# Pooled attention and a top-1 mixture of experts on one core: routing's loads on another queue, 26 filling products, four changes of order

## The chip, the core and the metric

The kernel runs on one core of a Trainium2 chip. The core has five engines with a queue of instructions each: TensorE (PE; its weight loads are shown as PEld), VectorE (DVE), ScalarE (ACT), GpSimd (POOL) and SyncE (SP, which here only issues DMAs and loads registers). Each queue runs in order; an instruction that waits for a semaphore holds all that stand behind it on its engine. ScalarE can issue DMAs as SP can. The metric is the device time of one execution in microseconds.

## What is computed

Inputs are q, k, v of 8 batches x 8 heads x 576 rows x 64, and a mixture of 8 experts of 512 x 1024 x 512. All is float32.

```python
k_p = k.reshape(B, H, Sp, pool, D).mean(axis=3)        # pool 8: 576 rows become 72
v_p = v.reshape(B, H, Sp, pool, D).mean(axis=3)
attn = softmax(scale * q @ k_p.T) ;  x = (attn @ v_p)  # 4608 tokens of 512
logits = x @ w_gate + modality_bias[modality_id]
e_idx = argmax(logits) ;  gate_w = softmax(logits)[e_idx]
out = gate_w * (relu(x @ w1[e_idx]) @ w2[e_idx])
```

## The kernel before, in words

**Attention** is 20 steps of two tiles of 128 query rows (the third of every five, the mixed step with `jj` None, has one tile, of two batches' remainders). Step n works in two halves w of four heads. Its parts are written as functions and called in an order written out by hand, in the loop over n from line 1097 on: `q_pe` (L679) transposes queries on PE into a PSUM tile `pq` of the pool `ps_tr`, which has two buffers, and `q_act` (L685) copies them to SBUF as `qt` on ACT; `s_pe` (L704, L698) makes scores `sc`; `s_dve` (L711, L714) subtracts the maximum on DVE; `s_act` (L726, L727) takes the exponential `pe` on ACT; `t_pe`, `t_act` (L733, L738) transpose it and copy it as `pt`; `t4_pe`, `t4_act` (L745, L752) do so for the remainders; `a_pe` (L768, L772) multiplies with the pooled values into `av`; `x_dve` (L791 to L801) normalises on DVE.

**Pooling** runs a batch or two ahead: `pool_k`, `pool_v` and their `_rest` fold eight rows on POOL (L458 to L460) or reduce on DVE (L463); `k_operand` (L502 to L511) transposes pooled keys on PE and copies them as `kt` on ACT; `v_operand` (L542 to L551) scales pooled values on ACT, and transposes them on PE as `pv`. Where they stand is set by the hooks `hook_0`, `hook_1`, `hook_q`, `hook_2`, `hook_3`, lists of functions for each step, run at five points of it.

**Routing** of a group of nine tiles is a list of small DVE operations, `route(g)`. They wait in the list `drip`, and `gap(n)` puts up to n of them between other DVE operations; an operation on PE in that list (`pe`, in the set `held`) stops `gap` until `release` takes it. POOL's `modality_terms` (L624 to L627), hooked at step 5, turns the modality and its bias into what L852 adds on DVE at step 6; these come by five DMAs of `load_routing` (L583, L585, L588), of 512, 256, 512, 256 and 128 rows of 32, 8, 32, 8 and 64 bytes.

**Loads.** Before the change SP issues all plain DMAs, in the order of `load_...` calls and of `step_loads`. Each DMA signals its landing on one of eight counters (DMAHW0 to DMAHW7), given out in turn to all DMAs in the order of the program, whichever engine issues them; the instruction that issues a DMA waits until the DMA before it on its counter has landed.

**Filling products** (`fill`, L494) are bf16 products of constants on PE that nobody reads.

**The experts** follow: slots of 256 tokens, gathered by POOL, with `first0` and `first_pair` (L193, L236, L240), `second` (L1436); the first expert's first products stand in the last attention steps. `first0` leaves its DVE part, the low part (L210), in the list `rests`, which `finish()` runs.

Of the kernel before, what the change touches and what calls it, by code (L numbers as in the profile page):

```python
# [9 lines left out]
F32 = mybir.dt.float32  # L10
F32R = mybir.dt.float32r
BF16 = mybir.dt.bfloat16
I32 = mybir.dt.int32
# [9 lines left out]
P = 128  # L23
# [11 lines left out]
def kernel(  # L35
# [303 lines left out]
    with ExitStack() as actx:  # L339
# [150 lines left out]
        def fill(n):  # L490

            t = ps_av.tile([P, 2, 512], F32, tag="av", name="fill")
            for _ in range(n):
                nc.tensor.matmul(t[:, 0, 0:P], iota_b, iota_b, start=True, stop=True)  # L494
# [44 lines left out]
        def v_operand(b):  # L539
            vp, vp4 = vps[b]  # L540
            dw, d4 = vw[b % NB], v4[b % NB]
            nc.scalar.activation(dw[:, :, 0, 0:HD], vp[:, 0:NPAIR, :], AF.Copy, scale=m_a)  # L542
            nc.scalar.activation(dw[:, :, 1, 0:HD], vp[:, 0:NPAIR, :], AF.Copy, scale=m_b)
            (nc.gpsimd if b else nc.vector).tensor_tensor(d4[:, :, 0:HD], vp4.rearrange("p (o d) -> p o d", o=1).to_broadcast([P, NPAIR, HD]),
                                    m4b.to_broadcast([P, NPAIR, HD]), op=ALU.mult)

            pv = ps_tr.tile([P, 3, P], F32, tag="tr", name=f"pv_{b}")
            for u in range(3):
                nc.tensor.transpose(pv[:, u, :], vp[:, 2 * u:2 * u + 2, :], ident)
            vts[b] = ap.tile([P, 3, P], F32, tag="vt", bufs=1, name=f"vt_{b}")  # L550
            nc.scalar.copy(vts[b], pv)  # L551

# [21 lines left out]

        RC = {}

        def load_routing():

            mod = ap.tile([P, NT, 2], I32, name="mod")
            mv = modality.bitcast(I32).rearrange("(n w) -> n w", w=2)  # L580
            for z in range(2):
                mz = mv.rearrange("(i z s) w -> z i s w", z=2, s=S)[z]
                nc.sync.dma_start(mod.rearrange("p (i t) w -> p i (t w)", t=GT)[:, :, 10 * z:10 * z + 8],  # L583
                                  mz[:, 0:512, :].rearrange("i (p j) w -> p i (j w)", j=4))
                nc.sync.dma_start(mod.rearrange("p (i t) w -> p i t w", t=GT)[64 * z:64 * z + 64, :, 4, :],  # L585
                                  mz[:, 512:S, :].rearrange("i p w -> p i w"))
            mb = ap.tile([P, 2, E], F32, name="mb")
            nc.sync.dma_start(mb.rearrange("p m e -> p (m e)"),  # L588
                              modality_bias.rearrange("m e -> (m e)").rearrange("(o x) -> o x", o=1).to_broadcast([P, 2 * E]))
            RC.update(mod=mod, mb=mb)  # L590

        def routing_constants():
            ids = ap.tile([P, NT], I32, name="ids")
# [53 lines left out]
        def gap(n=2):  # L647

            for _ in range(n):
                if drip and drip[0] not in held:  # L650
                    drip.pop(0)()
# [31 lines left out]
        def q_act(n, w):  # L683
            pq = pqs.pop((n, w))
            nc.scalar.copy(qts[n, w][:, 0:2 * len(steps[n][2]), :], pq)  # L685
# [18 lines left out]
                    nc.tensor.matmul(dst, qt[:, i, :], kt[b % NB][:, :, h * SPL:(h + 1) * SPL], start=True, stop=True)  # L704
            scs[n, w] = spare[w] = sc

        def s_dve(n, w):
            nh = 2 * len(steps[n][2])
            scv = scs.pop((n, w))[:, :, 0:nh * SPL].rearrange("p u (h s) -> p u h s", s=SPL)
            mx = ap.tile([P, 2, 4], F32, tag="mx", bufs=2, name=f"mx_{n}_{w}")[:, :, 0:nh]  # L710
            nc.vector.reduce_max(mx, scv, axis=AX.X)  # L711
            gap()
            sb = ap.tile([P, 2, 4 * SPL], F32, tag="sb", bufs=2, name=f"sb_{n}_{w}")
            nc.vector.tensor_tensor(sb[:, :, 0:nh * SPL].rearrange("p u (h s) -> p u h s", s=SPL), scv,  # L714
                                    mx.rearrange("p u (h o) -> p u h o", o=1).to_broadcast([P, 2, nh, SPL]), op=ALU.subtract)
            scs[n, w] = sb
# [31 lines left out]
        def t4_act(n):  # L748

            dst = pt4s[n]  # L750
            for z in range(len(steps[n][2])):
                nc.scalar.copy(pt4z[z][64 * z:64 * z + 64], dst[64 * z:64 * z + 64])  # L752
# [18 lines left out]
                for hs, y in halves:  # L771
                    nc.tensor.matmul(dst4[hs], pt4[:, hs], v4[y][:, 2 * u:2 * u + 2, :], start=False, stop=True)  # L772

        def x_dve(t):
            n, z = tile_step[t]
            g, gi = tile_group[t]
            av = avs.pop(t)
            mixed = steps[n][1] is None
            b = steps[n][0]
            if gi == 0:  # L780
                lgs[g] = late_p.tile([P, GT, H, E], F32, tag="lg", bufs=2, name=f"lg_{g}")
            xw = xbs[n if n < NX0 else NX0 + n % (len(xbs) - NX0)]
            xo = xw[:, z, 0:D]
            avv = av[:, :, 0:4 * VC].rearrange("p u (h x) -> p u h x", h=4)
            s8 = ap.tile([P, 2, 4], F32, tag="r", bufs=4, name=f"r_{t}")


            late = g >= EARLY_GROUPS and z == 1
            r = xw[:, z, RX:RX + H].rearrange("p (u h) -> p u h", u=2) if late else s8
            rb = r.rearrange("p u (h o) -> p u h o", o=1)  # L790
            nc.vector.tensor_scalar(s8, avv[:, :, :, VC - 1], float(POOL), 1e-9 * POOL, op0=ALU.mult, op1=ALU.add)  # L791
            if late:
                nc.scalar.copy(xo.rearrange("p (u h d) -> p u h d", u=2, h=4), avv[:, :, :, 0:HD])
            gap(1)
            nc.vector.reciprocal(r, s8)
            gap(1)
            nc.vector.tensor_tensor(lgs[g][:, gi].rearrange("p (u h) e -> p u h e", u=2), avv[:, :, :, HD:HD + E],
                                    rb.to_broadcast([P, 2, 4, E]), op=ALU.mult)
            if not late:
                for u in range(2):  # L800
                    nc.vector.tensor_tensor(xo[:, u * D // 2:(u + 1) * D // 2].rearrange("p (h d) -> p h d", h=4),  # L801
                                            avv[:, u, :, 0:HD], rb[:, u].to_broadcast([P, 4, HD]), op=ALU.mult)
            gap(2)

            if mixed:
                for y in range(2):
                    r0 = (b - 1 + y) * S + 512
                    stores.append(lambda y=y, r0=r0: nc.sync.dma_start(xs[r0:r0 + 64, :], xw[64 * y:64 * y + 64, 0, :]))
            elif z == 1:
                jj = steps[n][1]  # L810
                stores.append(lambda: nc.sync.dma_start(
                    xs[b * S:b * S + 512, :].rearrange("(p j) x -> p j x", j=4)[:, 2 * jj:2 * jj + 2, :], xw))
# [238 lines left out]

        step_loads = {}
        for n, fn, b in ((0, load_k, 2), (0, load_k4, 2), (0, load_v, 2), (0, load_v4, 2), (1, load_q, 2), (1, load_k, 3),
                         (1, load_v, 3), (1, load_k4, 3), (1, load_routing, None), (1, load_k, 4), (2, load_qmix, 1),
                         (2, load_v4, 3), (2, load_v, 4), (3, load_k4, 4), (4, load_q, 3), (4, load_k, 5), (4, load_v4, 4),
                         (4, load_v, 5), (5, load_k4, 5), (5, load_k, 6), (6, load_q, 4), (6, load_v4, 5), (6, load_v, 6),
                         (7, load_qmix, 2), (7, load_k4, 6), (7, load_k, 7), (9, load_q, 5), (9, load_v4, 6), (9, load_v, 7),
                         (10, load_k4, 7), (11, load_q, 6), (11, load_v4, 7), (12, load_qmix, 3), (14, load_q, 7)):
            step_loads.setdefault(n, []).append((fn, b))
# [11 lines left out]
        k_operand(0, 0)  # L1071
        q_pe(0, 0)
        q_act(0, 0)
        fill(6)
        s_pe(0, 0)
        fill(14)
# [1 line left out]
        s_dve(0, 0)  # L1078
        token_ids()
        k_operand(0, 1)  # L1080
        q_pe(0, 1)
        q_act(0, 1)
        pool_v(0)
        gate_operand()
        fill(8)
        s_act(0, 0)

        def run(hook, n):
            for fn in hook.get(n, ()):
                fn()  # L1090

        def finish():
            while rests:
                rests.pop(0)()

        due = False
        for n in range(N + 1):
            has, nxt, nxt2 = n < N, n + 1 < N, n + 2 < N
            old = steps[n - 1][2] if n else ()
# [13 lines left out]
            if old:  # L1113
                t4_pe(n - 1)
                t4_act(n - 1)
            if n == N:
                run(hook_3, N - 1)
            if ahead:
                t_pe(old[1])
                t_act(old[1])  # L1120
            if n == 2:
                a_pe(old[0])
            run(hook_1, n)
            if old and n != 2:
                a_pe(old[0])
            if has:
                s_dve(n, 1)
            finish()
            if n == 0:
                q_pe(1, 0)  # L1130
# [7 lines left out]
                q_act(n + 1, 0)  # L1138
            if nxt:
                q_pe(n + 1, 1)  # L1140
            run(hook_q, n)
            if old:
                x_dve(old[0])
            if n == N - 2:
                finish()
            gap(2)
            if nxt and n:
                q_act(n + 1, 1)
            if has:
                s_act(n, 1)  # L1150
            if n == 0:
# [587 lines left out]
```

## Time and profile before

| | us |
|---|---|
| median of 3 runs (579.84 to 583.59) | 581.89 |
| the profiled execution | 581.18 |
| its span, first to last instruction | 579.5 |
| mean granted TensorE clock | 0.996 |

The profile's page gives busy shares by engine, the chain of waits that ended last, and groups of instructions; the trace gives each engine's instructions in order of time, with what ended the idle time before them. Busy times of PE are modelled and hide short gaps, so idle time on PE is read from the rows that name a releaser and from the chain. A releaser "DMA x" is the landing of a DMA to x. Times inside the trace count from the span's start; the attention steps end at about 179 us.

### The profile page before, as it was taken

To read this page: it belongs to the slowest core of one execution; us is meant where nothing else is said; L and a number is where in the kernel's file an instruction comes from. 1 tells how busy PE (TensorE), PEld (TensorE's weight loads), DVE (VectorE), ACT (ScalarE), POOL (GpSimd) and SP (SyncE) were. 2 spreads that over 40 slices of the span, in tenths; PEclk is the share of its full clock that TensorE was granted. 3 is DMA by queue.
4 is the path that set the end of the run, shared out by engine and by line. 5 is a ranking of instruction groups with operands and counts; after the bars stand their busy time and mean duration, and the time that the engine had idled before them with its cause. 6 is when DMAs were issued, how large, how long until landed. Compare 5 with 4: busy or idle time off the path is not lost.

```text
span 579.5 us, 12256 instructions
## 1 busy us (share of the span) xinstructions
PE 562.1 (97%) x3487; PEld 494.5 (85%) x3487; DVE 372.7 (64%) x947; ACT 270.7 (47%) x656; POOL 183.6 (32%) x292
## 2 busy tenths in 40 slices
PE   4999999999999999999999999999999999999996
PEld 4889889899898888888888888888888888888894
DVE  5887888778878786567455446855455588455311
ACT  2667667789752443334333336533333474334210
POOL 6679987854201302202202102022112113212102
PEclk9899999999999999999999999999999999999999
DMA  8998999994431533232232277233234853242001
GB/s 249 279 332 251 358 334 281 338 274 164 166 94 43 153 101 111 79 105 94 92 110 95 89 236 244 93 114 94 87 114 129 241 205 108 91 133 74 26 21 56
DMA packets 80940, 90.69 MB, mean 157 GB/s; under 512 B 17935, under 2 KB 56335, under 8 KB 80848
## 3 DMA queue, kind: packets, MB, share of 16 engines
q1 hardware_dynamic: 74928, 70.14, 39.3%
q0 software_dynamic: 5920, 19.44, 10.3%
q8 instruction: 43, 0.70, 0.5%
q14 instruction: 49, 0.40, 0.3%
HBM read 115.72 MB, written 28.62 MB: 249 GB/s over the span
## 4 chain that ended last, share of the span: by engine, by line
PE 90%; DVE 3%; DMA 2%; ACT 2%; issue 1%; SPq 1%; POOLq 0%; ACTq 0%; DVEq 0%
PE op L1436 34%; PE hp L236 20%; PE hp L240 10%; PE av L768 6%; PE sc L704 4%; PE av L772 3%; PE hp L193 3%; PE pq L679 3%; PE pp L733 2%; PE ph L193 2%; DMA q<-in_q_dram 2%; DMA out_dram<-obw,slw 1%; PE sc L698 1%; PE pk L502 1%; PE sc L561 1%
## 5 line engine op out<-in xcount | busy, mean ns | idle before, releaser
L236 PE MATMUL hp<-xhl,hl 128*128 128x512 f32 (+1 forms) x512 | 146.5, 388 | 0.1
L1412 POOL DMA_INDIRECT out_dram<-ob,sidx x34 | 35.4, 1041 | 275.6 <-DVE ob L1406 204.7
L257 DVE TENSOR_TENSOR ht<-ht,hp 128x256 f32<-128x256 f32 x128 | 52.9, 419 | 99.7 <-ACT ht L256 88.0
L256 ACT COPY ht<-hp 128x256 f32<-128x256 f32 x128 | 47.1, 372 | 129.8 <-PE hp L236 124.4
L1436 PE MATMUL op<-hl,hx 128*128 128x512 f32 x429 | 103.5, 389 | 0.0
L236 PEld LDWEIGHTS hp<-xhl,hl 128*128 128x128 f32 x512 | 87.0, 188 | 10.3 <-issue 0.5
L1436 PEld LDWEIGHTS op<-hl,hx 128*128 128x128 f32 x429 | 80.4, 188 | 16.3
L240 PEld LDWEIGHTS hp<-xhl,hl 128*128 128x128 f32 x512 | 78.1, 189 | 9.9
L240 PE MATMUL hp<-xhl,hl 128*128 128x256 f32 (+1 forms) x512 | 80.7, 280 | 0.0
L1436 PE MATMUL op<-hl,hh 128*128 128x512 f32 x256 | 78.8, 389 | 0.0
L1436 PEld LDWEIGHTS op<-hl,hh 128*128 128x128 f32 x256 | 48.0, 188 | 9.8
L1436 PE MATMUL op<-hl,hlo 128*128 128x512 f32 x128 | 49.8, 389 | 0.0
L768 PE MATMUL av<-vw,pt 128*128 128x146 f32 (+1 forms) x320 | 48.9, 292 | 0.7 <-DVE xb L801 0.6
L151 POOL DMA_INDIRECT xg<-xs,gidx x36 | 38.0, 1054 | 17.3 <-issue 10.1
L768 PEld LDWEIGHTS av<-vw,pt 128*128 128x128 f32 (+1 forms) x320 | 39.6, 180 | 2.5 <-ACT pt L752 0.8
L704 PE MATMUL sc<-kt,qt 128*128 128x144 f32 x256 | 37.9, 292 | 0.4 <-ACT qt L685 0.4
L262 DVE SCALAR_TENSOR_TENSOR hx<-ht,hx 128x256 fp32r<-128x256 f32 x64 | 27.1, 425 | 16.1 <-DVEq L1441 14.3
L262 DVE SCALAR_TENSOR_TENSOR hlo<-ht,hh 128x256 fp32r<-128x256 f32 x64 | 27.0, 424 | 16.1 <-DVEq L1441 13.7
L704 PEld LDWEIGHTS sc<-kt,qt 128*128 128x128 f32 x256 | 34.1, 195 | 0.8 <-issue 0.6
L711 DVE TENSOR_REDUCE mx<-sc 128x8 f32<-128x576 f32 (+1 forms) x40 | 27.6, 691 | 6.8 <-PE sc L704 6.3
L260 ACT ACTIVATE hx<-ht 128x256 fp32r<-128x256 f32 x64 | 26.5, 420 | 10.1 <-DVE ht L257 10.0
L772 PE MATMUL av<-vw,pt 128*128 128x146 f32 (+1 forms) x160 | 30.3, 291 | 0.2
(281 smaller groups left out, 899.5 us busy)
## 6 DMA issues: line engine op xcount, KB each, us to landing
raw<-in_moe_w_dram SPq DMA_DIRECT2D x256, 256.0 KB
scr<-xg SPq DMA_DIRECT2D x35, 256.0 KB
xs<-xb SPq DMA_DIRECT2D x16, 528.0 KB
k<-in_k_dram SPq DMA_DIRECT2D x7, 1024.0 KB
v<-in_v_dram SPq DMA_DIRECT2D x7, 1024.0 KB
q<-in_q_dram SPq DMA_DIRECT2D x7, 1024.0 KB
y<-scr SPq DMA_DIRECT2D x108, 64.0 KB
v<-in_v_dram SPq DMA_DIRECT2D x16, 128.0 KB
```

What stands on the lines that cost most here:

```text
L151: nc.gpsimd.indirect_dma_start(out=x, out_offset=None, in_=xs[0:rows, :], in_offset=IndirectOffsetOnAxis(idx[:, col:col + 1].bitcast(U32), 0),
L193: nc.tensor.matmul(ph[:, 0:width], hl[f][:, w, d * P:(d + 1) * P], ab[:, 1 - x, d, 0:width], start=(n == 0 and d == 0), stop=(n == 2 and d ...
L236: nc.tensor.matmul(ph[:, :, 0:n], hl[g][:, 0, d * P:(d + 1) * P], ab[:, :, d, 0:n], start=(d == 0), stop=(d == ND - 1))
L240: nc.tensor.matmul(ph[:, 1, 0:n], hl[g][:, 1, d * P:(d + 1) * P], ab[:, 1, d, 0:n], start=False, stop=False)
L256: nc.scalar.copy(hts[g % 2], hp[g % 2][:, 0:SLOT])
L257: nc.vector.tensor_add(hts[g % 2], hts[g % 2], hp[g % 2][:, SLOT:2 * SLOT])
L262: nc.vector.scalar_tensor_tensor(hlo, hts[g % 2], 0.0, hh.bitcast(F32), op0=ALU.max, op1=ALU.subtract)
L704: nc.tensor.matmul(dst, qt[:, i, :], kt[b % NB][:, :, h * SPL:(h + 1) * SPL], start=True, stop=True)
L768: nc.tensor.matmul(av[hs, u, 2 * VC * gg:2 * VC * (gg + 1)], pt[:, c, hs], vw[y][:, c].rearrange("p a x -> p (a x)"), start=(gg == 0), sto ...
L772: nc.tensor.matmul(dst4[hs], pt4[:, hs], v4[y][:, 2 * u:2 * u + 2, :], start=False, stop=True)
L1412: nc.gpsimd.indirect_dma_start(out=out[:, :], out_offset=IndirectOffsetOnAxis(idx.bitcast(U32), 0), in_=ob, in_offset=None, bounds_check=N ...
L1436: nc.tensor.matmul(ot, l[:, ts_], hl[f][:, w, D:2 * D], start=(f == 0 and n == 0), stop=(f == NF - 1 and n == 2))
```

## The change

Routing's five loads leave SP: three functions issue them on ScalarE, at four places. `fill(16)` is put ahead of `q_pe(0, 1)`, `fill(10)` between the transposes of `v_operand(0)`. `finish()` is also called ahead of `s_dve` in the last step. `q_act(n + 1, 1)` is called right behind `q_pe(n + 1, 1)`. `gap` is left out of `s_dve` and the first `x_dve` of the step QUIET, which is 7. In step 4, as in step 2, the old tile's `a_pe` comes ahead of `hook_1` (there: `v_operand(2)`).

```diff
             for u in range(3):
                 nc.tensor.transpose(pv[:, u, :], vp[:, 2 * u:2 * u + 2, :], ident)
+                if b == 0 and u == 0:
+                    fill(10)
...
-        def load_routing():
...
+        def load_mod(z):
...
+            nc.scalar.dma_start(RC["mod"].rearrange("p (i t) w -> p i (t w)", t=GT)[:, :, 10 * z:10 * z + 8],
+                                mz[:, 0:512, :].rearrange("i (p j) w -> p i (j w)", j=4))
+        def load_mod4(z):
...
+            nc.scalar.dma_start(RC["mod"].rearrange("p (i t) w -> p i t w", t=GT)[64 * z:64 * z + 64, :, 4, :],
+                                mz[:, 512:S, :].rearrange("i p w -> p i w"))
+        def load_bias():
...
-        def s_dve(n, w):
+        def s_dve(n, w, fill_in=True):
...
-            gap()
+            gap(2 * fill_in)
...
-            gap(1)
+            gap(1 * fill_in)
             nc.vector.reciprocal(r, s8)
-            gap(1)
+            gap(1 * fill_in)
...
-                         (1, load_v, 3), (1, load_k4, 3), (1, load_routing, None), (1, load_k, 4), (2, load_qmix, 1),
+                         (1, load_v, 3), (1, load_k4, 3), (1, load_k, 4), (2, load_qmix, 1),
...
         q_act(0, 0)
+        load_mod(0)
+        load_bias()
+        load_mod4(0)
         fill(6)
...
         k_operand(0, 1)
+        fill(16)
         q_pe(0, 1)
...
         s_act(0, 0)
+        load_mod(1)
...
+        QUIET = s1_of[1] + 3
...
+            if n == 1:
+                load_mod4(1)
...
-            if n == 2:
+            if n in (2, 4):
                 a_pe(old[0])
             run(hook_1, n)
-            if old and n != 2:
+            if old and n not in (2, 4):
                 a_pe(old[0])
+            if n == N - 1:
+                finish()
             if has:
-                s_dve(n, 1)
+                s_dve(n, 1, n != QUIET)
...
                 q_pe(n + 1, 1)
+            if nxt and n:
+                q_act(n + 1, 1)
             run(hook_q, n)
...
-                x_dve(old[0])
+                x_dve(old[0], n != QUIET)
...
-            if nxt and n:
-                q_act(n + 1, 1)
```

ScalarE's queue at the start, before; `kt` is the key operand, `qt` a query copy, `pe` an exponential, `vw` the value operand.

```order
L685 COPY qt_0_265<-pq_0_266 128x512 [waits PE_49]
L510 COPY kt_133<-pk_1_310 64x192 [waits PE_49]
L511 COPY kt_133<-pk_1_310 64x192
L685 COPY qt_1_315<-pq_1_316 128x512 [waits PE_49]
L726 ACTIVATE pe_345<-sb_0_303 128x2x2x128 [waits DVE_49]
L727 ACTIVATE pe_345<-sb_0_303 128x2x32
L685 COPY qt_0_366<-pq_0_367 128x512 [waits PE_49,Activation_49]
L542 ACTIVATE vw_137<-vp_167,m_a 128x4x64 [waits DVE_49,Pool_49]
```

The same place now.

```order
L693 COPY qt_0_267<-pq_0_268 128x512 [waits PE_49]
L585 DMA mod<-in_moe_modality_id_dram 128x4x8 [waits DMAHW6_49]
L597 DMA mb<-in_moe_modality_bias_dram 128x16 [waits DMAHW7_49]
L592 DMA mod<-in_moe_modality_id_dram 64x4x2 [waits DMAHW0_49]
L510 COPY kt_133<-pk_1_315 64x192 [waits PE_49]
L511 COPY kt_133<-pk_1_315 64x192
L693 COPY qt_1_337<-pq_1_338 128x512 [waits PE_49]
L734 ACTIVATE pe_367<-sb_0_308 128x2x2x128 [waits DVE_49]
L735 ACTIVATE pe_367<-sb_0_308 128x2x32
L585 DMA mod<-in_moe_modality_id_dram 128x4x8 [waits DMAHW5_49]
L693 COPY qt_0_389<-pq_0_390 128x512 [waits PE_49,Activation_49]
L542 ACTIVATE vw_137<-vp_167,m_a 128x4x64 [waits DVE_49,Pool_49]
```

Four DMAs stand here that did not; each has a wait on a DMA's counter, and the copies and exponentials behind it come after that wait. The fifth (`load_mod4(1)`) stands in step 1, ahead of a `t_act`.

SP's queue from the load of batch 1's keys on, before.

```order
L357 DMA k_197<-in_k_dram 128x4x512 [waits DMAHW5_49]
L364 DMA k_1_199<-in_k_dram 64x512 [waits DMAHW6_49]
L395 DMA qm_201<-in_q_dram 64x8x64 [waits DMAHW7_49]
L395 DMA qm_201<-in_q_dram 64x8x64 [waits DMAHW0_49]
L372 DMA v_216<-in_v_dram 128x4x512 [waits DMAHW1_49]
L378 DMA v_1_218<-in_v_dram 64x1x512 [waits DMAHW2_49]
L378 DMA v_1_218<-in_v_dram 64x1x512 [waits DMAHW3_49]
L390 DMA q_221<-in_q_dram 128x8x256 [waits DMAHW4_49]
L357 DMA k_348<-in_k_dram 128x4x512 [waits DMAHW5_49]
```

The same place now.

```order
L357 DMA k_199<-in_k_dram 128x4x512 [waits DMAHW5_49]
L364 DMA k_1_201<-in_k_dram 64x512 [waits DMAHW1_49]
L395 DMA qm_203<-in_q_dram 64x8x64 [waits DMAHW2_49]
L395 DMA qm_203<-in_q_dram 64x8x64 [waits DMAHW3_49]
L372 DMA v_218<-in_v_dram 128x4x512 [waits DMAHW4_49]
L378 DMA v_1_220<-in_v_dram 64x1x512 [waits DMAHW6_49]
L378 DMA v_1_220<-in_v_dram 64x1x512 [waits DMAHW7_49]
L390 DMA q_223<-in_q_dram 128x8x256 [waits DMAHW0_49]
L357 DMA k_371<-in_k_dram 128x4x512 [waits DMAHW2_49]
```

The order is the same; the counters have moved on, because ScalarE's loads took some in between. Batch 1's keys (`k_199`) have counter 5; before, the next to use that counter was batch 2's keys on SP, now it is ScalarE's second `load_mod`.

PE's queue in the last attention step, around the first expert's third and fourth first products (`ph_2`, `ph_3`), before.

```order
L193 MATMUL ph_2_2540<-xhl_86,hl_1955 128x256 x11
L768 MATMUL av_2554<-vw_138,pt_2515 128x146 x2
L772 MATMUL av_2554<-vw_140,pt_0_135 128x2x73 [waits Activation_49]
L768 MATMUL av_2554<-vw_138,pt_2515 128x146 x2
L772 MATMUL av_2554<-vw_140,pt_0_135 128x2x73
L733 MATMUL pp_2566<-ident,pe_2401 128x128 [waits DVE_49]
L733 MATMUL pp_2566<-ident,pe_2401 128x128 x3
L193 MATMUL ph_3_2583<-xhl_86,hl_2069 128x256 [waits Activation_49]
```

The same place now.

```order
L193 MATMUL ph_2_2568<-xhl_86,hl_1983 128x256 x11
L776 MATMUL av_2582<-vw_138,pt_2543 128x146 x2
L780 MATMUL av_2582<-vw_140,pt_0_135 128x2x73 [waits Activation_49]
L776 MATMUL av_2582<-vw_138,pt_2543 128x146 x2
L780 MATMUL av_2582<-vw_140,pt_0_135 128x2x73
L741 MATMUL pp_2594<-ident,pe_2429 128x128 [waits DVE_49]
L741 MATMUL pp_2594<-ident,pe_2429 128x128 x3
L193 MATMUL ph_3_2611<-xhl_86,hl_2097 128x256 [waits DVE_49]
```

The fourth products now wait for DVE's low part, which moved ahead of `s_dve`, and no longer for ScalarE's copy. On DVE that low part is the only operation that changes its place; no routing operation does.

## Rows read from the trace of the kernel before

**Rows 1.** The page: busy time by engine, and the chain that ended last.

```profile
PE 562.1 (97%) x3487; PEld 494.5 (85%) x3487; DVE 372.7 (64%) x947; ACT 270.7 (47%) x656; POOL 183.6 (32%) x292
...
PE 90%; DVE 3%; DMA 2%; ACT 2%; issue 1%; SPq 1%; POOLq 0%; ACTq 0%; DVEq 0%
```

**Rows 2.** Windows: length, busy by engine, PE clock, DMA share, GB/s.

```profile
10.00:20.00 10.00, 7.18 (x54) 6.59 (x55) 8.29 (x13) 3.14 (x9) 6.21 (x13) 0.83 1.12 283
```

**Rows 3.** Chain of waits, start of the kernel: start, length, what.

```profile
5.75 8.84 DMA q<-in_q_dram
...
14.63 0.96 PE pq L679 x4
...
16.45 2.02 PE sc L704 x8
18.47 0.45 PE pq L679 x4
...
21.98 0.66 PE pp L733 x4
```

**Rows 4.** Timeline of ScalarE: start, length, what, [idle before, releaser].

```profile
12.60 0.31 ACT L510 COPY kt<-pk 64x192 f32<-64x192 f32 x1 [2.40 <-PE pk L507]
...
16.64 0.31 ACT L727 ACTIVATE pe<-sb 128x64 f32<-128x64 f32 x1
19.01 0.58 ACT L685 COPY qt<-pq 128x512 f32<-128x512 f32 x1 [2.05 <-PE pq L679]
...
25.89 0.58 ACT L738 COPY pt<-pp 128x512 f32<-128x512 f32 x1 [1.50 <-PE pp L733]
```

**Rows 5.** Timeline of SP's queue, routing's loads.

```profile
39.80 0.58 SPq L583 DMA_DIRECT2D mod<-in_moe_modality_id_dram  x1
...
42.36 2.86 SPq L585 DMA_DIRECT2D mod<-in_moe_modality_id_dram  x1
...
47.10 0.56 SPq L357 DMA_DIRECT2D k<-in_k_dram  x1
```

**Rows 6.** Waits of SP's queue to 60 us: total, times, longest.

```profile
SPq L357 <- DMA k<-in_k_dram: 1.4, 1, 1.4
```

**Rows 7.** Timeline of POOL: folds of batch 0's remainders, batch 1's keys, modality terms.

```profile
11.77 0.73 POOL L458 TENSOR_TENSOR v<-v 128x256 f32<-128x256 f32 x1 [2.95 <-DMA v<-in_v_dram]
...
21.17 1.26 POOL L458 TENSOR_TENSOR k<-k 128x512 f32<-128x512 f32 x1 [1.86 <-DMA k<-in_k_dram]
...
62.31 0.68 POOL L627 TENSOR_TENSOR sc<-mq,mb 128x288 f32<-128x288 f32 x1
```

**Rows 8.** Windows at the two changes of the clock, columns as in rows 2.

```profile
14.50:15.00 0.50, 0.37 (x3) 0.37 (x4) 0.43 (x3) 0.00 (x0) 0.42 (x2) 0.84 1.07 304
...
18.20:18.40 0.20, 0.20 (x3) 0.20 (x3) 0.00 (x0) 0.00 (x0) 0.20 (x2) 0.86 1.35 156
```

**Rows 9.** DMA from 46 to 48 us: packets, MB, share of 16 engines.

```profile
q1 hardware_dynamic: 997, 0.14, 43.3%
```

**Rows 10.** Timeline of DVE in step 6.

```profile
63.66 0.88 DVE L852 TENSOR_TENSOR bias_all<-bias_all,sc 128x288 f32<-128x288 f32 x1
```

**Rows 11.** Timeline of PE: fills at full clock, then idle in steps 4, 8, 19.

```profile
11.40 0.94 PE L494 MATMUL fill<-iota_b 128*128 128x128 bf16 x14
...
46.91 0.41 PE L549 MATMUL pv<-ident,vp 128*128 128x128 f32 x2 [0.26 <-DVE vp L463]
...
81.90 0.63 PE L679 MATMUL pq<-ident,q 128*128 128x128 f32 x4 [0.43 <-ACT qt L685]
...
165.87 1.68 PE L193 MATMUL ph<-xhl,hl 128*128 128x256 f32 x12 [0.68 <-ACT pt L738]
```

**Rows 12.** Chain of waits in step 13.

```profile
117.53 0.11 PE pk L502
...
117.78 0.31 ACT kt L510
```

**Rows 13.** Timeline of DVE in step 19: the low part.

```profile
165.15 0.41 DVE L210 SCALAR_TENSOR_TENSOR h<-ph,h 128x256 fp32r<-128x256 f32 x1
```

More of the change, by code (lines that the diff above doesn't have):

```diff
@@ L575 @@
         RC = {}
-        def load_routing():
-            mod = ap.tile([P, NT, 2], I32, name="mod")
+        RC.update(mod=ap.tile([P, NT, 2], I32, name="mod"), mb=ap.tile([P, 2, E], F32, name="mb"))
+        def load_mod(z):
             mv = modality.bitcast(I32).rearrange("(n w) -> n w", w=2)
[L581 to L590, printed above, removed]
+            mz = mv.rearrange("(i z s) w -> z i s w", z=2, s=S)[z]
+            nc.scalar.dma_start(RC["mod"].rearrange("p (i t) w -> p i (t w)", t=GT)[:, :, 10 * z:10 * z + 8],
+                                mz[:, 0:512, :].rearrange("i (p j) w -> p i (j w)", j=4))
+        def load_mod4(z):
+            mv = modality.bitcast(I32).rearrange("(n w) -> n w", w=2)
+            mz = mv.rearrange("(i z s) w -> z i s w", z=2, s=S)[z]
+            nc.scalar.dma_start(RC["mod"].rearrange("p (i t) w -> p i t w", t=GT)[64 * z:64 * z + 64, :, 4, :],
+                                mz[:, 512:S, :].rearrange("i p w -> p i w"))
+        def load_bias():
+            nc.scalar.dma_start(RC["mb"].rearrange("p m e -> p (m e)"),
+                                modality_bias.rearrange("m e -> (m e)").rearrange("(o x) -> o x", o=1).to_broadcast([P, 2 * E]))
         def routing_constants():
@@ L772, in a_pe, with x_dve @@
                     nc.tensor.matmul(dst4[hs], pt4[:, hs], v4[y][:, 2 * u:2 * u + 2, :], start=False, stop=True)
-        def x_dve(t):
+        def x_dve(t, fill_in=True):
             n, z = tile_step[t]
```

## The prediction

> **What bounds the kernel now.** I read the page first: PE is busy for 97% of the span, and 90% of the chain that ended last is PE's own work; DVE, ACT and DMAs hold the rest [rows 1]. So what an edit saves counts only where PE stood idle or where the chain leaves PE. Next I read windows for places where PE is not full. The worst in the attention steps is 10 to 20 us: PE has 7.18 of 10 us, the granted clock is 0.83 on average, and the DMA engines are full (share 1.12) [rows 2]. The chain says why: the second half of batch 0's queries lands at 14.59 (5.75 + 8.84), PE resumes with `pq` at 14.63, scores end at 18.47 (16.45 + 2.02), and ScalarE's work leads to `pp` at 21.98 [rows 3]. The clock falls to half (1.2 GHz) between 14.5 and 15.0, after the engine stood idle waiting for those queries, and is full again (2.4 GHz) from 18.2 to 18.4 [rows 8]. Last I read each queue in order of time around every moved instruction, for its neighbours and their slack.
>
> **Routing's loads, SP's side.** SP loses the stretch from 39.80 to 47.10 us, 7.30 us of issuing and waiting [rows 5]. I give that nothing: what follows there are loads for later batches, which POOL folds a step or more ahead of their use; if that cover were gone, later keys would come up to 7.3 us late, which this change does not do.
>
> **ScalarE's side, first three loads.** They stand behind the copy of the first queries; ScalarE was idle for 2.40 us before the next key copy at 12.60 [rows 4]. The counters they wait on belong to batch 0's v remainders (6 and 7) and its first v pairs (0); the remainders landed at 11.77 at the latest, since POOL folds them then [rows 7], and the v pairs before the queries of 14.59. One issue took 0.58 us on SP [rows 5], so three end at about 13.5 to 14.7, and the two key copies (0.31 us each) at 15.3 at the latest, about when the copy of the second queries is due. Cost taken: 0; upper end 0.5 us.
>
> **The fourth load is the term that matters.** `load_mod(1)` stands behind the second exponential, which ended at 16.95 (16.64 + 0.31), and ahead of the query copy that ran at 19.01 [rows 4]. It waits on counter 5, that of batch 1's keys. Those land at 21.1: POOL, idle until then, starts to fold them at 21.17 [rows 7]. SP shows what such a wait does: its only wait for keys, 1.4 us, was for the DMA that shared this counter [rows 6]. ScalarE is now the waiter, and behind it in its queue stand the query copy, the value operands, the exponentials and through them PE's `pp`. The copy starts at about 21.1 + 0.58 + 0.04 = 21.7 and no longer at 19.01: +2.7 us. What ScalarE did from 19.01 to 21.98 is a chain without slack [rows 3, 4], so all of it shifts. Ends: SP's `qm` loads, of 256-byte rows, are now issued later (they wait on counters of v and gate loads), so keys may land up to 1.5 us earlier; or the small packets delay them. For those I have one price: 997 packets, nearly all small, took 43.3% of 16 engines for 2 us [rows 9], 0.433 x 2 x 16 / 997 = 13.9 ns each; the three early loads have 512 + 128 + 256 = 896, so 896 x 13.9 / 16 = 0.8 us at most. The term lies between +1.2 and +3.5; I take 2.7, the landing that the row shows.
>
> The Trainium skill (DMA: Bandwidth & Descriptors, section Queues, rings and completion order) says that each DMA engine takes turns between the queues it has work for, and its section on issuing engines that another issuer saves only issue time, since the transfers share the same 16 engines; by that rule the 0.8 us would be paid in full and the total would be 583.4, by the row of the landing alone it is 582.6. No run here shows two hardware queues yet.
>
> The fifth load, in step 1, waits on the counter of batch 1's key remainders, landed by then, and stands where ScalarE was idle for 1.50 us [rows 4]; its 0.58 is covered.
>
> **Filling products.** One costs 0.94 / 14 = 0.067 us at full clock [rows 11]: 16 are 1.07 us, 10 are 0.67. The 16 lie in the 2.07 us in which PE waits for queries, so they cost nothing and may keep the clock. At full clock the pieces between 14.63 and 18.92 would be up to 1.7 us shorter, half of the 3.4 us at 1.2 GHz [rows 8]. I count this as 0 all the same, since ScalarE, held to 21.7, is what PE waits for then; it would count only without that hold. The 10 lie in that hold too. But PE now idles from about 19.3 to 22, longer than the idle time after which the clock fell before, so I expect a second fall; most of such a stretch passes while ScalarE works off its 2.9 us, so I take +0.25, between 0 and 1.7.
>
> **Orders.** The queries' copy ahead of the key copies: in step 8 PE waited 0.43 us for it [rows 11], and its PSUM buffer is now free in time: -0.4. In step 13 the chain passes through it and the copy can start when `pq` ends, about 0.2 us ahead of the key copy at 117.78 [rows 12]: -0.2. Elsewhere it is not on the chain: 0. In step 4 `a_pe` fills the 0.26 us that PE waits for DVE's fold [rows 11]; `pv` is late next, and has slack until `v_gate`: -0.3, between 0 and -0.4. The low part in step 19: PE's next `ph` waited 0.68 us for ScalarE's copy [rows 11]; now it takes the buffer that the low part frees, which ended at 165.56 (165.15 + 0.41) [rows 13] and now ends before `s_dve`, at about 164.1: -0.6, between 0 and -0.7. "Four routing operations" do not move: at step 7 the list's head is a held operation, so `gap` had nothing to put there, and DVE's order is unchanged: 0. Sum of the orders: -1.5, between -0.4 and -1.7.
>
> **The sum.** 2.7 + 0.25 - 1.5 = +1.45 us. Nothing takes the shift back: DVE's `bias_all` at 63.66 follows POOL's terms, done at 62.99 [rows 7, 10], with 0.67 us to spare, so a late PE finds POOL ready, and the experts behind are PE's work. On the profiled execution's 581.18 this is **582.6 us**, 0.7 above the median of the runs before (581.89), whose own spread is 3.7.
>
> **Rivals.**
> - *The hold is short.* Keys land before ScalarE comes to `load_mod(1)`, or soon after. For it: their packets were spread over 12 to 21 us among small ones that now come later. Against it: POOL's idle time ends with them at 21.17 [rows 7]. Then the early part gains up to 1.0 (the 1.7 us of clock less what the v folds behind 16.7 us keep), and POOL's 0.67 us before `bias_all` [rows 7, 10] is the most that survives: 581.18 - 0.6 - 1.5 = 579.1.
> - *ScalarE is held by the issuing itself: slower.* SP's longest small load took 2.86 us [rows 5]. If all five take that on ScalarE, the three early ones end at 11.7 + 8.6 = 20.3, key and query copies at 21.5 where they ended at 16.2 (+5.3), the fourth adds 2.86 less some 2 us of cover, the fifth 2.86 - 1.50 = 1.4, the clock 0.9: 581.18 + 5.3 + 0.9 + 1.4 + 0.9 - 1.5 = 588.2. It decides from some 2 us an issue on, where the early three pass the queries' landing. For it: 2.86 was measured with full DMA engines, as they are from 10 to 20. Against: ScalarE's own queue is empty, and the other kind of load took 0.58 in the same state.
> - *The hold, and the orders give nothing*, because ScalarE's shifted work meets them: 581.18 + 2.7 + 0.25 + 0.7 = 584.8, with the early packets' delay.
>
> **How the numbers follow.** Forecast 0.58, short hold 0.25, long issues 0.07, no savings 0.10. The range goes from the short hold to the forecast's upper bounds: 578.8 to 585.4; it leaves out the long issues and the tails. A measurement of this kernel tells about 1% (5.8 us) from no change; only the long issues pass that, and a faster time of that size has no source in the trace: faster 0.03, same 0.91, slower 0.06.
>
> **What would show it.** In the changed kernel's trace: ScalarE idle in front of the query copy behind the exponentials until POOL's first fold of batch 1's keys, and that copy at 21 to 22; `pp` at 24 to 25; no half clock from 15 to 18, perhaps one after 21; in step 8 no wait of `pq` for `qt`; in step 19 no wait of `ph` for `pt`; DVE's routing operations where they were. I am wrong if the copy runs by 19.5, if the key copies of the first step come after 16, or if the time is outside the range.

## The result: slower by about 5 us, and the profile after

The changed kernel takes 586.53 us (median of 8 runs, 584.46 to 588.18) against 581.62 for the kernel before on the same chip: ratio 1.0095, 95% interval [1.0074, 1.0115]. The forecast was 582.6, in a range that ended at 585.4. The profiled execution has 586.53 us and a span of 584.8, 5.3 more than before. By the bar that the prediction set (about 1% tells from no change) this is the "same" that it gave 0.91; its interval tells it from no change all the same. Two of the twelve executions of the first experiment (630 and 1993 us) stand far from all others and are left out of its time and ratio.

The profile's page of the changed kernel, where [rows 1] had 97% and a chain that was 90% PE:

```profile
PE 564.0 (96%) x3513; PEld 496.8 (85%) x3513; DVE 373.4 (64%) x947; ACT 271.3 (46%) x656; POOL 184.0 (31%) x292
...
PE 83%; DVE 7%; DMA 6%; ACT 2%; issue 1%; SPq 0%; POOLq 0%; ACTq 0%; DVEq 0%
```

DMA's share of the chain went from 2 to 6%. Half of that rise is the start (17.7 us of DMA up to 32 us, 8.8 before), the other half a stretch in the experts where the chain goes through transfers (9.5 us between 400 and 500, none before). DVE's went from 3 to 7%, nearly all of it between 66 and 186 us. A share of the chain is not time lost: PE can be busy beside it. The chain of waits of the changed kernel, 8 to 32 us (start, length, what), answers to [rows 3]:

```profile
10.83 10.24 DMA k<-in_k_dram
...
21.09 0.39 ACTq L585
...
21.58 0.59 ACT qt L693
...
22.21 0.66 PE pq L687 x4
22.87 1.21 PE sc L712 x8
24.08 1.12 PE pg L563 x6
```

The chain no longer goes through the queries of 14.6 us. It goes through the landing of batch 1's keys at 21.07 (10.83 + 10.24), ScalarE's `load_mod(1)`, and the query copy behind it. ScalarE's timeline says the same, with 5.25 us of idle time where [rows 4] had 2.05:

```profile
16.02 0.31 ACT L735 ACTIVATE pe<-sb 128x64 f32<-128x64 f32 x1
21.09 0.39 ACTq L585 DMA_DIRECT2D mod<-in_moe_modality_id_dram  x1
21.58 0.58 ACT L693 COPY qt<-pq 128x512 f32<-128x512 f32 x1 [5.25 <-DMA k<-in_k_dram]
```

Windows of the changed kernel (length, PE's busy time, the granted clock, DMA share, GB/s) show the price that follows: the first fall of the clock, of [rows 8], is gone, and another comes behind the hold.

```profile
16.00:18.00 2.00, 2.00 (x23) 1.00 1.01 351
...
20.00:22.00 2.00, 0.00 (x0) 1.00 1.26 183
...
23.00:24.00 1.00, 1.00 (x9) 0.75 1.04 385
24.00:25.00 1.00, 1.00 (x7) 0.50 1.09 318
...
27.00:28.00 1.00, 1.00 (x10) 1.00 1.19 307
```

Matching PE's groups one by one in two traces gives by how much PE is late (+) or early (-) against the kernel before, here at seven places, named by the start before. A column that changes from one row to the next has lost or gained something between them. The last two columns are experiments told below.

| start before, place | after | fill(8) | loads alone |
|---|---|---|---|
| 18.31, `pq` ahead of the held copy | -1.58 | -1.23 | -1.82 |
| 19.65, `pq` behind it | +2.56 | -0.84 | -1.44 |
| 23.46, step 1, remainders' transpose | +3.92 | -0.84 | -1.44 |
| 66.53, `av`, ahead of the first routing steps | +3.67 | -1.02 | -1.24 |
| 69.46, step 7 | +4.61 | -1.14 | -1.23 |
| 107.98, step 12 | +5.38 | -0.20 | -1.25 |
| 185.64, end of the attention's stretch | +4.89 | -0.67 | -1.25 |

So of 4.9 us at the end of this stretch 2.56 are the hold and 1.36 come right behind it. 0.94 are lost in step 7 and 0.84 in step 12; some 0.8 come back, 0.25 of it ahead of step 7 and 0.5 behind step 12. (Counted by the loop's n, as in the prediction, the second place is step 12; the expectations below call it step 10.) The span is 5.3 us longer and not 4.9, most of it by a wait of PE of 0.56 us in the experts.

The mean granted clock of the eight executions says something that one trace can't: the fastest, 584.46 us, had 1.000, so no fall of the clock at all, and the slowest, 588.18, had 0.991. In that execution, without a fall, the changed kernel lies inside the predicted range.

### The profile page after: what moved, and what is told of

Its sections match the earlier page's. It is cut to its first block, busy times and chain, and to the rows that moved or that the text cites. A ratio compares the mean times of both kernels' runs of the same rounds, so it can differ in the third digit from the quotient of the medians.

```text
span 584.8 us, 12314 instructions
## 1 busy us (share of the span) xinstructions
PE 564.0 (96%) x3513; PEld 496.8 (85%) x3513; DVE 373.4 (64%) x947; ACT 271.3 (46%) x656; POOL 184.0 (31%) x292
## 4 chain that ended last, share of the span: by engine, by line
PE 83%; DVE 7%; DMA 6%; ACT 2%; issue 1%; SPq 0%; POOLq 0%; ACTq 0%; DVEq 0%
PE op L1454 32%; PE hp L236 19%; PE hp L240 10%; PE av L776 5%; PE sc L712 4%; DMA k<-in_k_dram 3%; PE hp L193 3%; PE av L780 3%; PE pq L687 2%; PE pp L741 2%; DMA xg<-xs,gidx 1%; PE ph L193 1%; DMA out_dram<-obw,slw 1%; DVE mx L719 1%; DVE sb L722 1%
```

## Experiments: is it the hold, and what makes it

**The second load later on ScalarE.**

```diff
         s_act(0, 0)
-        load_mod(1)
...
             if n == 1:
+                load_mod(1)
                 load_mod4(1)
```

> The changed kernel with one edit: ScalarE's second `load_mod` stands in step 1, right ahead of `load_mod4(1)`, and no longer behind the second exponential. It then takes another counter, and SP's load of batch 1's v remainders takes the one of batch 1's keys. Theory (ScalarE was held by the landing of the keys; that and the fall of the clock behind it are 3.9 us): the query copy that ran at 21.58 runs before 19.2, PE has no fall of the clock after 21 us, the time is 581.5 to 583.5; SP now waits for the keys until about 21 with the v remainders, which may cost up to 2 us later on, inside that range. Rival (ScalarE's loads cost by their issue or by their packets, wherever they stand): the copy stays behind 20.5 or the time at 585 or more.

581.5 us (median of ten), ratio 1.0002 [0.9977, 1.0027]: the whole loss is gone, and the rival with it. The query copy ran at 17.36. What the theory had feared also came: SP's load of the v remainders now had the keys' counter. SP's row, DVE's row and PE's row of this kernel:

```profile
21.79 1.20 SPq L378 DMA_DIRECT2D v<-in_v_dram  x2
```

```profile
27.63 1.06 DVE L463 TENSOR_REDUCE vp<-v 128x64 f32<-128x512 f32 x1 [1.14 <-DMA v<-in_v_dram]
```

```profile
30.91 0.33 PE L753 MATMUL sc<-ident,pe 128*128 128x128 f32 x1 [1.04 <-DVE sb L722]
```

The hold had moved to SP, whose load waited for the landing of the keys; DVE waited 1.14 us for v and PE 1.04 for DVE, which took back 1.1 us of an early gain of 1.44.

**The loads alone**: the kernel before with the five loads at the changed kernel's places, no fills, no orders.

> The kernel before with the loads alone moved to ScalarE, at the changed kernel's four places; no fills, no orders. Without the fills the second `load_mod` takes counter 4 (the gate weights) and no longer 5, and batch 1's large v load on SP takes 5 and waits for batch 1's keys. Theory: what costs is the wait on the counter of a late transfer, whoever makes it; so ScalarE is hardly held here (the query copy at 18.5 to 19.5, as before), while SP issues that v load at 21 and no longer at 16, POOL's fold of it (27.5 before) comes 2 to 4 us later, and the time is 582.5 to 585.5. Rival (ScalarE's own issuing or its place is what costs): the copy comes at 20.5 or later here too, with SP's v load at 16 to 18.

581.6 us, ratio 1.0007 [0.9990, 1.0024]. With counter 4 ScalarE issued the load at 17.09 and copied at 17.57; SP issued the v load at 20.71, and the fold came at 26.16, not late at all, so the time is below the expected range: the cost that was expected of SP's wait did not come. While SP waited the DMA engines had little to do (share 0.34 from 20 to 22 us, 1.19 before). PE stays 1.2 to 1.8 us early from the start to 185 us.

**The loads back on SP**, with the fills and orders kept:

```diff
+                         (1, load_v, 3), (1, load_k4, 3), (1, load_routing, None), (1, load_k, 4), (2, load_qmix, 1),
...
-        load_mod(0)
-        load_bias()
-        load_mod4(0)
...
-        load_mod(1)
...
```

> The changed kernel with routing's five loads back on SP at their old place; the fills and the four changes of order stay. Theory: no hold on ScalarE; the early part keeps full clock and PE is 1 to 1.5 us early at 17 us, of which the later waits for v and keys take most back; the orders' savings are given back in the same step (low part, step 8), so the time is 580.5 to 582.5. Rival A (the orders do save what the prediction gave them, 1.5 us, and only the loads hid it): 579 to 580.3. Rival B (the orders or the fills themselves cost, as DVE's waits of 0.8 us in steps 7 and 10 suggest): 583 or more.

581.56 us, ratio 1.0007 [0.9986, 1.0028], as the theory had it. Neither the loads nor the rest of the change costs 5 us alone; together they do. In the profiled execution PE came 1.45 us early to step 7 and left step 8 1.09 late: behind its waits in step 7 (0.81 and 0.62 us) the clock fell, to 0.50 from 71 to 73 us.

**One number in a fill.** ScalarE's load has counter 4 without the fills, 5 with them. The counters are given out when the program is built, and eight products fewer on PE are enough to swap `load_mod(1)` with SP's v load:

```diff
-        fill(16)
+        fill(8)
         q_pe(0, 1)
```

> The changed kernel with `fill(8)` in place of `fill(16)`, nothing else. With eight products fewer on PE the second `load_mod`, at the same place on ScalarE, is given counter 4 (the gate weights' load) and no longer 5; SP's large v load of batch 1 takes 5. Theory (which counter the load gets decides, not its place and not the fills' work): the query copy behind it runs at 17 to 19 and no longer at 21.58, PE reaches step 1's remainder transpose at 22 to 23 instead of 27.38, and the time is 581 to 583. Rival (the place on ScalarE, or a cost of the loads there, is what lost 4 us): the copy at 21 or later, the time at 586 or more.

580.84 us, ratio 0.9988 [0.9971, 1.0006], where the changed kernel has 586.53 and 1.0095. The time is just below the expected range. The load has the same place on ScalarE. ScalarE's and SP's queues in this kernel:

```profile
17.69 0.39 ACTq L585 DMA_DIRECT2D mod<-in_moe_modality_id_dram  x1
18.18 0.59 ACT L693 COPY qt<-pq 128x512 f32<-128x512 f32 x1 [1.49 <-PE pq L687]
```

```profile
16.43 1.28 SPq L395 DMA_DIRECT2D qm<-in_q_dram  x2
21.14 0.37 SPq L372 DMA_DIRECT2D v<-in_v_dram  x1
```

The copy waits for PE, no longer for keys; now SP waits for them (it was done with the issue before its v load at 17.71, and issued that load at 21.14). This settles the cause of the hold: the wait on the keys' counter, not the place and not the issuing.

**Without the other fill** (`fill(10)` left out, counter still 5):

> The changed kernel without `fill(10)`. The second `load_mod` keeps counter 5. Theory: ScalarE is held as in the changed kernel, the query copy runs at 21 to 22, the clock falls behind it, the time is 585.8 to 587.5; ten products that end 3 us before PE is wanted change nothing. Rival (fills have cost PE time of their own, 0.7 us): 585.5 or less.

588.76 us, ratio 1.0125 [1.0098, 1.0153]: the hold stays (copy at 21.68), as expected, but the time is above the range. The one profiled execution took 586.57 and follows the changed kernel to 0.14 us at 185 us, so its trace does not show what the others lost. Their granted clock points to a longer fall: 0.991 and 0.992 in the four executions from 588.75 on, 0.994 and 0.995 in the two at 586.6. Where it fell in those four is not traced. In another run with the hold (the old place of the query copies, below) the clock was at 0.50 until 31 us, and PE was 5.96 us late at step 1 and 6.88 from there on.

**The clock's part.** `fill(60)` in place of `fill(10)`:

> The changed kernel with `fill(60)` in place of `fill(10)` in the first value operand: at 0.067 us each they keep PE busy for 4.0 us, over most of the time in which ScalarE is held. The hold itself stays. Theory (of the 3.9 us lost by step 1, 2.6 are the hold and 1.3 the fall of the clock that PE's idle time brings behind it): the clock stays full from 21 to 28 us, the query copy still runs at 21 to 22, PE's first remainder transpose of step 1 comes 1.2 to 1.4 us earlier than the changed kernel's 27.38, and the time is 584.7 to 585.6. Rival (the clock's fall costs nothing there, because PE waits for ScalarE anyway, as the prediction had it to within 0.25): 586.3 or more, the transpose within 0.4 us of 27.38.

ScalarE was held as before (its copy at 21.21), and the clock stayed full:

```profile
22.00:24.00 2.00, 2.00 (x18) 1.00 1.06 362
24.00:26.00 2.00, 1.89 (x16) 1.00 1.12 282
```

The transpose of step 1 came at 25.65 (the second row) and no longer at 27.38 (the first, of the changed kernel).

```profile
27.38 0.27 PE L753 MATMUL sc<-ident,pe 128*128 128x128 f32 x1
```

```profile
25.65 0.27 PE L753 MATMUL sc<-ident,pe 128*128 128x128 f32 x1
```

Of these 1.73 us 0.36 are the keys' earlier landing, 1.37 the clock: the rival, which was the prediction's 0.25, falls. The median fell less than expected, to 586.0 (ratio 1.0064 [1.0038, 1.0090]), between the two expected ranges. In the trace PE is 1.5 us ahead of the changed kernel at 185.64, and only 0.7 of that is left at the end.

## Experiments: where the orders' savings went

**A small operation on DVE.** Step 12 of the changed kernel: DVE's, POOL's and PE's rows.

```profile
110.56 1.02 DVE L889 TENSOR_SCALAR sm<-sm 128x9 f32<-128x9 f32 x1
```

```profile
110.28 1.27 POOL L458 TENSOR_TENSOR v<-v 128x512 f32<-128x512 f32 x1
```

```profile
112.19 0.33 PE L753 MATMUL sc<-ident,pe 128*128 128x128 f32 x1 [0.37 <-DVE sb L722]
```

The same operation and fold in the kernel before:

```profile
106.03 0.17 DVE L881 TENSOR_SCALAR sm<-sm 128x9 f32<-128x9 f32 x1
```

```profile
106.02 1.30 POOL L458 TENSOR_TENSOR v<-v 128x512 f32<-128x512 f32 x1
```

An operation on 9 numbers a partition lasts 1.02 us and ends at 111.58, as the fold beside it does (111.55); before, it lasted 0.17. The subtraction `sb` is behind it, and PE behind that. In step 7 of the changed kernel it met the scaling of the pooled values on POOL (L544) and ended with it, and PE waited 0.81 us; before (the first row), it lasted 0.33 there.

```profile
68.67 0.33 DVE L881 TENSOR_SCALAR sm<-sm 128x9 f32<-128x9 f32 x1
```

```profile
72.77 0.89 DVE L889 TENSOR_SCALAR sm<-sm 128x9 f32<-128x9 f32 x1
```

```profile
73.02 0.61 POOL L544 TENSOR_TENSOR vw<-vp,m 128x256 f32<-128x256 f32 x1
```

```profile
74.07 0.33 PE L753 MATMUL sc<-ident,pe 128*128 128x128 f32 x1 [0.81 <-DVE sb L722]
```

The Trainium skill (SBUF — State Buffer, section Who interferes with whom) says that DVE and GpSimd share one port pair of SBUF, which an instruction holds exclusively until its end, and that a `tensor_scalar` can be of the kind that needs it; the rows agree, except that starts 0.01 us apart do not tell which of the two came first. The test takes the operation out:

```diff
-            add(lambda: V.tensor_scalar_add(sm, sm, 1e-9))
+            add(lambda: None)
```

> The changed kernel without the addition of 1e-9 to the sums of the routing softmax (`sm`, four small DVE operations in all; its place in the list stays, empty). Theory (this operation, 0.16 us alone, lasted 0.89 and 1.02 us in steps 7 and 10 because DVE had to wait for a POOL fold that held a port both use): the subtraction behind it comes earlier by 0.7 to 0.9 us in those two steps, PE's waits of 0.81 and 0.37 plus 0.41 us for `sb` and `pt` go, and the time falls by 1.0 to 1.6 us to 585. Rival (DVE is late for another reason, such as later inputs, and the long operation only fills a wait): PE's two waits stay and the time stays at 586.5.

585.2 us, ratio 1.0074 [1.0045, 1.0102]. Against the changed kernel PE gained 0.89 in step 7 and 0.90 in step 12, and lost 0.46 at the start of step 9 in a wait for `sb`. The median fits the theory, but part of it may be the start: in the profiled execution the clock fell ahead of the hold (0.50 from 11 to 14 us), not behind it, and PE came to step 7 1.8 us earlier than in the changed kernel. The gains within the steps are what shows the mechanism.

**The query copies back at their place.**

> The changed kernel with the copies `q_act(n + 1, 1)` back at their old place. Theory (the move saves 0.58 in step 8 and loses it again there in waits for `sb`; and in step 10 it lets POOL's fold start 0.26 us earlier, ahead of DVE's `sm`, which then waits a whole fold: 0.85, with 0.17 in step 13): in step 10 `sm` lasts under 0.3 us and PE does not wait for `sb`, PE waits 0.4 us for `qt` in step 8 again, the time falls by 0.8 to 1.2 us to 585.5. Rival (the move gains its 0.6 and step 10 is late for another reason): 587, and PE's waits in step 10 stay.

Step 12 of this kernel, DVE and POOL:

```profile
113.75 0.17 DVE L889 TENSOR_SCALAR sm<-sm 128x9 f32<-128x9 f32 x1
```

```profile
113.74 1.31 POOL L458 TENSOR_TENSOR v<-v 128x512 f32<-128x512 f32 x1
```

The fold starts 0.01 us ahead of `sm` and not 0.28, and `sm` goes through: PE gains 0.85 in step 12, as expected, and loses 0.37 in step 18. The 0.17 of step 13 does not show: the move gains it, and the next step's transposes lose it again. From step 7 to 185 us the move cost some 0.5 us net. This execution was late for another reason too, but the other runs leave no doubt on step 12: in each of the seven kernels with the move and with `sm` PE lost 0.84 to 0.86 there, whether it came early or late, and POOL had waited 0.56 us for ScalarE's `vg` copy ahead of the fold; in the kernel before and the loads alone POOL waited 0.84 us, and PE lost nothing. The moved query copy, which had run between ScalarE's routing exponential and that `vg` copy, now runs ahead of both. Two more expectations failed. In step 8 the wait for `qt` did not come back; it is absent in the loads alone too, without any order changed, so the move never was what removed it. And the time did not fall (587.42, ratio 1.0085 [1.0054, 1.0116]). Its executions had granted clocks of 0.990 to 0.995, and in the profiled one (591.04) the clock fell for longer at the start than in the changed kernel; one of its windows:

```profile
27.00:28.00 1.00, 1.00 (x7) 0.50 1.23 297
```

**The low part and the tile of step 4, undone together.**

```diff
-            if n in (2, 4):
+            if n == 2:
...
-            if n == N - 1:
-                finish()
```

> The changed kernel with two orders undone, which stand far apart and are read apart in the trace: the low part of step 19 and `a_pe` of step 4. Theory (both savings come back as another wait in the same step: the products behind wait 0.7 us for `x_dve`, which the low part delays; the transposes behind `pv` wait for ScalarE's later `vt`): in step 19 PE waits 0.6 to 0.9 us ahead of `ph` and no longer ahead of the next `av`, in step 4 it waits 0.2 to 0.4 us ahead of `pv`; the shift of PE against the kernel before is the same on either side of both steps to 0.25 us, and the time stays at 586.2 to 586.9. Rival (they save 0.9 together, as predicted): 587.4.

587.55 us, ratio 1.0091 [1.0064, 1.0118]. The time is above the expected range, at the rival's 587.4; the ratio, each against the kernel before on its own chip, is the changed kernel's 1.0095. The trace decides: at 185.64 PE is 4.88 us late, 4.89 in the changed kernel. Step 19 with the low part ahead of `s_dve` (changed kernel, PE, then DVE):

```profile
169.84 1.65 PE L193 MATMUL ph<-xhl,hl 128*128 128x256 f32 x12
172.21 0.74 PE L776 MATMUL av<-vw,pt 128*128 128x146 f32 x4 [0.71 <-ACT hl L1021]
```

```profile
171.31 0.74 DVE L809 TENSOR_TENSOR xb<-av,r 128x256 f32<-128x256 f32 x2
```

and with it undone:

```profile
170.75 1.68 PE L193 MATMUL ph<-xhl,hl 128*128 128x256 f32 x12 [0.68 <-ACT pt L746]
```

`ph` waits 0.68 us for the copy in one order, `av` 0.71 in the other: its instruction waits for ScalarE and DVE, and DVE's `xb`, which the low part pushes back, ends at 172.05 (171.31 + 0.74). The releaser that the row names, a cast of the expert's weights, is not what `av` reads; and in step 7, where the row names `xb`, PE went on as long behind the end of `xb` (75.31, 75.46) as here (172.05, 172.21). Undone, PE is 0.93 later at `ph` and 0.85 earlier at `av`: 0.08 net, and that is gone at the next transposes. In step 4 the undone order has a wait of 0.43 us for `vp` again, and behind the step the changed order has gained 0.05.

**Two versions meant to beat both.** The loads alone without the 1e-9, and the changed kernel with `fill(8)`, the query copies at their old place and no 1e-9.

> The kernel before with the loads alone on ScalarE (as in the run of the loads alone, where ScalarE was not held and PE came 1.25 us earlier to the end of the attention) and without the addition of 1e-9. Theory: no wait that is left on DVE's chain in steps 7 and 10 is that operation's here, since it took 0.33 and 0.17 us there, so little is gained: 580.5 to 581.6. Rival (DVE's small operations set the pace in every routing step): 579.5 or less.

> The changed kernel with `fill(8)` for `fill(16)`, with `q_act(n + 1, 1)` back at its old place and without the addition of 1e-9. Theory: no hold, no collision of `sm` with a fold in steps 7 and 10; what is left is the early gain of 1.2 to 1.4 us at the start, of which the experts keep a part: 580 to 581.5, below the kernel before by 0.3 to 1.5. Rival (every gain in the attention is eaten by the next wait, also across steps): 581.6 or more.

581.0 us (0.9989 [0.9972, 1.0006]) and 580.93 us (0.9992 [0.9973, 1.0012]): neither is told apart from the kernel before. Both are inside the expected ranges. In the first PE ends the attention 1.27 us early. Part of such a gain is taken by a wait in the experts. In most of these traces PE waits 0.35 to 1.75 us for DVE once, at 472 to 482 us; in the kernel before and in that with the second load later it does not. What DVE waits for (here the kernel without the 1e-9) is a gathered tile:

```profile
473.23 0.76 DVE L304 TENSOR_TENSOR xg<-xg 128x256 f32<-128x256 f32 x2 [2.15 <-DMA xg<-xs,gidx]
```

## Why the prediction was wrong

- **The hold: right.** Place and cause were as written. The copy was forecast at 21.7 and ran at 21.58; +2.7 was taken, +2.56 measured. To a tenth this is luck: over the kernels here POOL began to fold these keys between 20.2 and 22.3 us. For the same reason the small packets' price stays open. The 0.8 us that the prediction got by the Trainium skill's rule of turns between queues (DMA: Bandwidth & Descriptors, section Queues, rings and completion order) does not show in this trace, where the keys landed at 21.07, but SP's `qm` loads also went out later here (16.52 for 14.04), which could hide it. ScalarE issued at 0.38 to 0.69 us a load, so the rival of long issues fell.
- **The second fall of the clock: the step that failed first.** The prediction saw it and took +0.25 between 0 and 1.7, because "most of such a stretch passes while ScalarE works off its 2.9 us". Measured are 1.36 in the changed kernel and 1.37 by the long fill. From 22.21 on the chain is PE's own work: ScalarE stayed ahead of PE, so every half-speed product counted in full. Sizes differ between executions, as the granted clocks show; in one of the eight there was none.
- **The orders: the step that failed by most.** -1.5 was taken. The low part gave nothing and step 4 0.05: each had its next wait in the same step. Step 8's -0.4 had nothing to do with the order, and what PE gained there was lost again, to 0.14 us, by the next step's transposes in every kernel. Step 13's 0.2 was gained (0.17) and lost in the same way. The query copies let a fold start ahead of `sm` in step 12, +0.85, for which the prediction had no term. The signs that it named came, no wait of `pq` in step 8 and none of `ph` in step 19; a wait that is gone was not a gain.
- **Step 7: not foreseen.** +0.94, from a collision of the same kind. POOL was delayed by 2.5 us (its modality terms ended at 65.51 and not at 62.99, [rows 7]) and DVE by 3.8 to 4.1; so DVE's `sm` met another operation of POOL than before. It is the distance of the two that counts, not the lateness: with the loads back on SP `sm` came 1.0 us early and POOL 2.6, the same distance, and PE lost the same 0.94. The slack of 0.67 us that the prediction checked was the wrong kind of check: nothing waited for POOL's result, DVE's small operation waited for POOL's to end.
- **"Four routing operations" moved nothing, SP's 7.30 us were worth nothing, and the 16 fills cost PE nothing**: as written. But the fills decided through the build which load got the keys' counter. The prediction compared only the two finished orders, so it had the counter right and its dependence on the fill unseen.

Put right, the sum is 2.56 + 1.36 + 0.94 + 0.84 = 5.7, less some 0.8 that come back: the 4.9 measured. Of the 3.9 us by which the forecast was short, 1.1 are the clock, 1.5 the savings that did not come, 1.8 the two collisions and 0.4 the experts, less those 0.8 and 0.1 of the hold. The nearest rival was the hold with no savings, at 584.8; it lacked the clock's 1.1 and the two collisions, and had 0.7 for packets that the trace does not show.

## What to carry to other kernels

When a DMA moves to a busy engine, look up which earlier transfer its completion counter belongs to and when that lands: here the next DMA on the counter of the large load waited for it in every run with the loads on ScalarE, whoever issued it, and that should be a queue with nothing urgent behind it. Behind a hold of the engine that feeds PE, reckon with a fall of the clock: it cost 1.36 us here, and the run that kept PE busy did not pay it. A saved wait counts only if the next input is in time too, so read the next two releasers before giving an order a price.

## What the runs showed of the hardware that was not expected

- A `tensor_scalar` of 128x9 on DVE took 0.17 us when it began with POOL's fold and 1.02 when it began 0.28 us behind it: it ended with the fold. Seven kernels show the second, three the first.
- With SP held for the keys, the v load that it issued 4.7 us later (20.71 for 16.04) was folded 1.4 us earlier (26.16 for 27.52). That the wait sped it up is not shown: with the loads back on SP it was issued at 15.84 and folded at 25.37, so two executions of one order of loads differ by 2 us here.
- The clock's fall behind the same hold did not have one size: 1.36 us in the changed kernel, and PE 5.96 late at step 1 instead of 3.92 in the run with the query copies at their old place, where it was at 0.50 until 31 us. In the run without the 1e-9 there was none behind the hold; the clock had fallen from 11 to 14 us, and PE was 2.03 late at step 1.
